# A ConvNeXt-V2 block on one core: two-bank expansion tiles, the evacuation last in a slot, statistics one slot later, and means aggregated by bn_stats

## The chip, the core and the metric

The kernel runs on one core of a Trainium2 chip. The metric is the device time of one execution in microseconds (us). Inputs and outputs are in bf16, and sums are formed in f32.

## The reference

The input `x` is one image of 512 x 512 pixels with 96 channels. All of it is one ConvNeXt-V2 block:

```python
out = sum over i, j of xp[:, i:i+H, j:j+W, :] * dw[i, j]     # 3x3 depthwise, zero padding
h = layernorm(out)                                           # over the 96 channels, eps 1e-5
h = gelu_tanh(einsum('bhwc,ce->bhwe', h, w1))                # 96 -> 384
gx = sqrt((h * h).sum(axis=(1, 2)) + 1e-6)                   # over all pixels, one per channel
nx = gx / (gx.mean(axis=-1) + 1e-6)
h = grn_gamma * (h * nx) + grn_beta + h
return x + einsum('bhwe,ec->bhwc', h, w2)                    # 384 -> 96
```

`gx` needs the squares of all activated values of the whole image before the last product can begin, so the kernel makes two passes.

## The kernel before

**Blocks and slots.** The image is cut into 128 blocks of four rows (2048 pixels). The first pass is one Python loop over slots `s`. In each slot several blocks are at different stages; a table filled by `put(slot, stage, block)` says which. Engines take their instructions in the order in which the loop issues them (the class `InOrder`, line 35, through which nearly every instruction goes; that is why the profile shows L35 for nearly all), so this order is written out by hand. In the steady part a slot does the following, each for another block.

- SP issues loads of `x` (`load_x`), reads of normalized rows (`stage_read`, `ynT`), writes of them (`stage_write`, `yn_dram`), the small row transfers of the layer norm (`stage_rows`, `stage_bcast`, tile `rbc`), and a third of a stored block (`store_next`).
- POOL: `stage_newton` (eight small operations for a batch of four blocks), `stage_norm` (`yn = y_bf * rbc`), `stage_sq` (`ysq = y_bf * y_bf`, of the block whose convolution was evacuated in the slot before), `stage_rstd` (four small operations for a batch).
- PE: the 3x3 convolution of block `s` as 72 matmuls on 64x32 tiles, issued in three bursts `conv(0)`, `conv(1)`, `conv(2)` into the three banks `Y3`; a PE drain follows `conv(0)`. `evac` on ACT copies `Y3` to `y_bf`. `stage_stats` takes 24 small matmuls (`rowsel`) over `y_bf` and `ysq`, the sums for the layer norm.
- PE and ACT: the expansion to 384 channels and the gelu of one block, 12 banks of 512 numbers, by `unit(bank, n)`: `n` banks are filled by matmuls of `w1p` and `ynT`, and one ACT instruction turns them to `g`.
- DVE: `turn_x` (two transposes of x, tile `xT`); `stage_moments` (reads the sums, then clears the bank); `squares`, `squares_rest` and `square_owed`, which issue one `bn_stats` on 512 numbers each into `bst`. `bn_stats` writes six numbers: count, mean and sum of squared deviations of the even and of the odd elements. The rest of the block is squared on PE by `gram_next`.

The PSUM banks: `banks(2)` is always banks 0 and 1, and `banks(1)` takes banks 2 and 3 in turn. `Y3` is banks 4 to 6, bank 7 holds the sums `S` and the gram matrix. In a slot with expansion the order is

```python
conv(0)
unit(0, 2); unit(2, 1); squares(0)
conv(1, False)
spread_out(); turn_x(s + 3)
unit(3, 1); unit(4, 2); squares(1); gram_next(1)
unit(6, 1); squares(2); unit(7, 1)
stage_turn; conv(2); evac(); gram_next(1)
unit(8, 2); unit(10, 1); stage_stats; unit(11, 1); stage_moments
squares_rest(2); square_owed()
```

**Aggregation.** Every 32 entries of `bst` (a group) are put together by three `bn_aggr`, one for each 128 channels, into mean and variance `mv`. `second_moments` turns these to sums of squares `parts`. After the loop the last group and the gram matrix are added and the scale for `w2` is formed; this is the gate between the passes.

**Second pass.** 14 tail blocks at the end of the first pass go through `mlp_tail`, with tiles of three banks. The output pass then recomputes, keeps or loads `g`, multiplies by the scaled `w2` and adds `x`.

Of the kernel before, what the change touches and what calls it, by code (L numbers as in the profile page):

```python
# [8 lines left out]
ALU = mybir.AluOpType  # L9
ACTF = mybir.ActivationFunctionType  # L10
AX = mybir.AxisListType
# [3 lines left out]
GRN_EPS = 1e-6  # L15
# [41 lines left out]
def kernel(  # L57
# [92 lines left out]
    NLAST = cm_quads(NBLK - 2) + cm_quads(NBLK - 1)  # L150
    GROUPS = [min(32, NENT - k) for k in range(0, NENT, 32)] + [NLAST]
    NACC = len(GROUPS)
    mv = consts.tile([128, NCH, NACC, 2], f32, name="mv")
    parts = consts.tile([128, NCH, NACC + 1], f32, name="parts")
    npx = consts.tile([128, NACC], f32, name="npx")
    grp = {}
    NYT = 6
    yn_ring = [prepool.tile([128, GR, W], bf16, name=f"ynT{i}") for i in range(NYT)]
# [25 lines left out]
    with ExitStack() as p1:  # L184
# [2 lines left out]
        ones = [0]  # L187

        def banks(n):
            if n == 2:  # L190
                return PS[:, 0:2, :]
            ones[0] += 1
            return PS[:, 2 + ones[0] % 2:3 + ones[0] % 2, :]

        threes = [0]

# [183 lines left out]
        def busy(n):  # L380
            for k in range(n):
                pe.matmul(Y3[:, k % NI, :], lhsT=zrow[:, :128], rhs=zrow[:], start=True, stop=True)
# [16 lines left out]
        n = 0  # L399
# [35 lines left out]

        def setup_rest():
            dve.memset(ones_f[:], 1.0)
            for k in range(NACC):
                dve.memset(npx[:, k:k + 1], float(GROUPS[k] * QW))
            dve.tensor_copy(out=gam[:], in_=gam_bf[:])  # L440

        def turn_x(b):
# [64 lines left out]
        def stage_sq(b, on_act):  # L507
            q = ysqpool.tile([128, NI, W], bf16, name="ysq")
            if on_act:
                act.activation(out=q[:], in_=ybf[b][:], func=ACTF.Square)  # L510
            else:
                pool.tensor_tensor(out=q[:], in0=ybf[b][:], in1=ybf[b][:], op=ALU.mult)
            ysq[b] = q
# [242 lines left out]
        def square_owed():  # L756
            while owed:
                owed.pop()()
# [10 lines left out]

        def aggregate(k):  # L770
            bst = bsts.pop(k)
            for j in range(NCH):
                dve.bn_aggr(out=mv[:, j, k, :], in_=bst[:, j, :GROUPS[k], :].rearrange("p a s -> p (a s)"))

        def combine(b):
            for k in sorted(bsts):
# [1 line left out]
                    aggregate(k)  # L778

        def second_moments(k0, k1):  # L780
            v, p = mv[:, :, k0:k1, :], parts[:, :, k0:k1]
            dve.tensor_tensor(out=p, in0=v[:, :, :, 0], in1=v[:, :, :, 0], op=ALU.mult)
            dve.tensor_tensor(out=p, in0=p, in1=v[:, :, :, 1], op=ALU.add)
            dve.tensor_tensor(out=p, in0=p, in1=npx[:, None, k0:k1].to_broadcast([128, NCH, k1 - k0]), op=ALU.mult)

        at = {}

# [6 lines left out]
        for k, (b0, n) in enumerate(BATCHES):  # L794
# [16 lines left out]
            for b in range(b0, b0 + n):  # L811
# [7 lines left out]
                put(m + is_whole(b), "combine", b)  # L819
                last_slot = m  # L820

        busy(FILL[1])
        turn_x(0)
        turn_x(1)
        turn_x(2)
        for s in range(last_slot + 1):
            get = lambda kind: at.get((s, kind), [])
            if s + 4 < NBLK:
                load_x(s + 4)
            for b in get("read"):  # L830
                stage_read(b)
            for b in get("write"):
                stage_write(b)
            for k in get("bcast"):
                stage_bcast(k)
            for k in get("rows"):
                stage_rows(k)
            store_next()
            for k in get("newton"):
                stage_newton(k, pool)  # L840
            for b in get("norm"):
                stage_norm(b)
            for b in get("sqp"):
                stage_sq(b, False)
            for k in get("rstd"):
                stage_rstd(k, pool)
            mlp = get("mlp")

            def spread_out():
                for k in get("spread"):  # L850
                    stage_spread(k)
                for b in get("norma"):
                    stage_norm(b, dve if b < 2 else pool)

            spare = not mlp and s % 2 == 1
            taps, evac = conv_taps(s, spare) if s < NBLK else ([], None)
            if mlp and mlp[0] >= TAIL0:
                assert not taps
                square_owed()
                mlp_tail(mlp[0], get)  # L860
            elif not mlp:
                if s + 3 < NBLK:
                    turn_x(s + 3)
                for f in taps:
                    f()
                if not spare:
                    spread_out()
                if evac:
                    evac()
                for b in get("sqa"):  # L870
                    stage_sq(b, True)
                for b in get("stats"):
                    stage_stats(b)
                for k in get("moments"):
                    stage_moments(k)
                if spare:
                    spread_out()
                for k in get("chain"):
                    stage_moments(k)
                    stage_chain(k)  # L880
                for k in get("turn"):
                    stage_turn(k)
                gram_next(2)
                square_owed()
            else:
                b = mlp[0]
                unit, squares, squares_rest = mlp_units(b)
                conv = lambda n, fence=True: taps[n](fence) if taps else None

                conv(0)  # L890
                unit(0, 2)
                unit(2, 1)
                squares(0)
                conv(1, False)
                spread_out()
                if s + 3 < NBLK:
                    turn_x(s + 3)
                unit(3, 1)
                unit(4, 2)
                squares(1)  # L900
                gram_next(1 if taps else 2)
                unit(6, 1)
                squares(2)
                unit(7, 1)
                for k in get("turn"):
                    stage_turn(k)
                conv(2)
                if evac:
                    evac()
                gram_next(1 if taps else 2)  # L910
                unit(8, 2)
                unit(10, 1)
                for b2 in get("stats"):
                    stage_stats(b2)
                unit(11, 1)
                for k in get("moments"):
                    stage_moments(k)
                squares_rest(2)
                square_owed()
                if is_whole(b):  # L920
                    owed.append(lambda f=squares_rest: f(3))
                grams.extend((b, c) for c in range(cm_quads(b) * QC, NQ * QC, 2 * E))
                if is_whole(b):
                    stores.extend((b, h) for h in range(3))
            if s == 0:
                setup_ynt()
            if s == 3:
                setup_mlp()
            if s == 4:
                setup_rest()  # L930
            for b in get("combine"):
                combine(b)
            if s == last_slot - 3:
                pc.close()
                late.xr = p2.enter_context(tc.tile_pool(name="xr", side="right", bufs=5))
                late.xb = p2.enter_context(tc.tile_pool(name="xb", side="right", bufs=3))
                late.gr = p2.enter_context(tc.tile_pool(name="gr", side="right", bufs=GRB))
                late.gl = p2.enter_context(tc.tile_pool(name="gld", side="right", bufs=2))
                late.o = p2.enter_context(tc.tile_pool(name="o", side="right", bufs=4))
            if s == last_slot - 2:  # L940
                for n in range(PRE):
                    load_xr(n, sp)
            if s == last_slot - 1:
                for n in range(3):
                    stage_xb(ORDER[n], pool, B2bc_f)
                second_moments(0, NACC - 1)
            if s == last_slot:
                for n in range(PRE):
                    load_rest(n, sp, sp)
# [5 lines left out]
        aggregate(NACC - 1)  # L955
        second_moments(NACC - 1, NACC)
        sums = gsm.tile([128, NCH], f32, name="sums")
        dve.tensor_reduce(out=sums[:], in_=parts[:, :, :NACC], axis=AX.X, op=ALU.add)
        for j in range(NCH):
            junk = bstpool.tile([128, 128], f32, name="junk")  # L960
            dve.scalar_tensor_tensor(out=junk[:], in0=gram[:, j, :], scalar=1.0, in1=ident_f[:],
                                     op0=ALU.mult, op1=ALU.mult, accum_out=parts[:, j, NACC:NACC + 1])
        ssq = gsm.tile([128, NCH], f32, name="ssq")
        dve.scalar_tensor_tensor(out=ssq[:], in0=sums[:], scalar=GRN_EPS, in1=parts[:, :, NACC],
                                 op0=ALU.add, op1=ALU.add)
        gi = gsm.tile([128, NCH], i32, name="gi")
        dve.tensor_scalar(out=gi[:], in0=ssq[:].bitcast(i32), scalar1=-0.5, scalar2=float(0x5F3759DF),
# [84 lines left out]
```

## Time and profile before

| What | Value |
|---|---|
| Three runs | 1476.99, 1479.7, 1480.79 us; median 1479.7 |
| The profiled execution: its span, which is also its time as given | 1480.8 us |
| Granted TensorE clock, mean | 0.994 |
| First pass, from the first y_bf to the last (start) | 12.1 to 883.7 us |
| Gate (last aggregation to scaled w2) | 967.1 to 973.5 us |
| Busy: PE, DVE, ACT, POOL | 1391.3, 1182.0, 1414.4, 1300.3 us |
| ACT, g of one bank, of two banks | x684, mean 701 ns; x342, mean 1115 ns |
| ACT, y_bf of three banks | x121, mean 1561 ns |
| DVE, bn_stats on 512 numbers | x1110, mean 672 ns |
| DVE, bn_aggr on 32 entries | x33, mean 978 ns |
| POOL, yn and ysq | x126, mean 3108 ns; x114, mean 2752 ns |

Means are lengths of single instructions. On ACT, PE and DVE the next one starts before the last has ended, so the price of an instruction on a full engine is the distance from its start to the next start, which the timeline shows; it is less than the mean length.

### The profile page before, as it was taken

How to read it: one execution, taken by the hardware profiler on the slowest of the kernel's cores; microseconds unless marked ns; L12 is line 12 of the kernel's file. 1: busy time of each engine (PE TensorE's matmuls, PEld its weight loads, DVE VectorE, ACT ScalarE, POOL GpSimd, SP SyncE). 2: the span in 40 equal slices, each digit the busy share in tenths (PEclk: the TensorE clock that was granted, in tenths of full speed). 3: DMA queues.
4: the chain of work that ended last, by engine and by line, in shares of the span. 5: the costliest groups of instructions: out<-in, count | busy, mean ns of one | idle time of the engine just before them, and what ended most of it. 6: DMA issues, size and time to landing. Idle time of an engine off the chain costs nothing.

```text
span 1480.8 us, 54225 instructions
## 1 busy us (share of the span) xinstructions
PE 1391.3 (94%) x23125; PEld 810.4 (55%) x23125; DVE 1182.0 (80%) x2135; ACT 1414.4 (96%) x1595; POOL 1300.3 (88%) x922
## 2 busy tenths in 40 slices
PE   8888999999999999999999997789999999999998
PEld 3434444444444444444444445467777777776776
DVE  7849989999999999999999987965555555555555
ACT  7888989999999999999999999999999999999997
POOL 3459889998998999998999987569999999999997
PEclk9999999999999999999999999999999999999999
DMA  5568788788888888888888866669999999999997
GB/s 180 179 205 255 241 253 280 228 271 260 260 248 264 258 264 255 276 253 254 263 258 266 263 216 195 195 225 409 366 359 402 417 416 413 419 410 417 411 412 282
DMA packets 167768, 433.08 MB, mean 292 GB/s; under 512 B 31558, under 2 KB 81318, under 8 KB 163046
## 3 DMA queue, kind: packets, MB, share of 16 engines
q1 hardware_dynamic: 151284, 326.04, 66.3%
q0 software_dynamic: 14880, 103.43, 17.6%
q8 instruction: 181, 2.97, 0.8%
q14 instruction: 61, 0.50, 0.1%
q10 hardware_dynamic: 1362, 0.15, 0.1%
HBM read 273.30 MB, written 156.22 MB: 290 GB/s over the span
## 4 chain that ended last, share of the span: by engine, by line
PE 30%; ACT 24%; DMA 19%; POOL 13%; DVE 6%; issue 4%; SPq 4%; POOLq 0%; ACTq 0%; DVEq 0%
PE PS L35 30%; ACT g L35 16%; DMA out_dram<-o_sb 9%; POOL yn L35 6%; ACT y_bf L35 5%; POOL ysq L35 5%; SPq L35 4%; DMA yn_dram<-yn 3%; DVE bst L35 3%; DMA xin<-in_x_dram 2%; DMA rbc<-r_dram 2%; DMA ynT<-yn_dram 1%; DMA g_dram<-g 1%; DVE o_sb L35 1%; ACT xT L35 1%
## 5 line engine op out<-in xcount | busy, mean ns | idle before, releaser
L35 ACT ACTIVATE g<-PS 128x512 bf16<-128x512 f32 (+2 forms) x1062 | 727.7, 864 | 16.5 <-PE PS L35 15.6
L35 DVE BATCH_NORM_STATS2 bst<-g 128x6 f32<-128x512 bf16 x1110 | 671.3, 672 | 35.4 <-ACT g L35 34.5
L35 PE MATMUL PS<-ynT,w1p 128*128 128x512 bf16 x2181 | 609.6, 381 | 23.6 <-ACT g L35 5.4
L35 ACT ACTIVATE gr<-PS 128x1536 bf16<-128x1536 f32 x360 | 498.5, 1459 | 18.8 <-PE PS L35 13.8
L35 POOL TENSOR_TENSOR yn<-y_bf,rbc 128x1536 bf16<-128x1536 bf16 x126 | 391.3, 3108 | 77.3 <-ACT rbc L35 21.9
L35 DVE TENSOR_TENSOR o_sb<-PS,xb 128x384 bf16<-128x384 f32 x512 | 277.3, 556 | 227.0 <-PE PS L35 190.1
L324 POOL TENSOR_TENSOR xb<-xr,B2c 128x1536 f32<-128x1536 bf16 x118 | 368.1, 3133 | 4.3 <-DVE o_sb L35 2.0
L35 PE MATMUL PS<-xT,Wq 64*32 64x511 bf16 (+1 forms) x9198 | 340.5, 389 | 26.2 <-ACT y_bf L35 8.1
L35 POOL TENSOR_TENSOR ysq<-y_bf 128x1536 bf16<-128x1536 bf16 x114 | 313.6, 2752 | 12.8 <-ACT y_bf L35 12.8
L35 PEld LDWEIGHTS <-w1p 128*128 128x128 bf16 x2181 | 171.6, 98 | 222.0 <-issue 133.4
L35 PEld LDWEIGHTS <-gr 128*128 128x128 bf16 x4296 | 212.1, 98 | 68.9 <-issue 12.0
L35 PE MATMUL PS<-W2s,gr 128*128 128x96 bf16 x4224 | 223.5, 206 | 8.2 <-DVE o_sb L35 8.0
L35 PEld LDWEIGHTS <-Wq 64*32 64x32 bf16 x9216 | 111.9, 90 | 193.3 <-issue 145.9
L35 ACT ACTIVATE y_bf<-PS 128x1536 bf16<-128x1536 f32 (+2 forms) x135 | 199.4, 1482 | 17.4 <-PE PS L35 13.3
L35 DVE STREAM_TRANSPOSE xT<-xin 128x576 f32<-128x576 f32 (+1 forms) x256 | 181.4, 748 | 8.1 <-DMA xin<-in_x_dram 8.1
L35 PEld LDWEIGHTS <-g 128*128 128x128 bf16 x1704 | 104.9, 98 | 86.3 <-issue 54.3
L35 PE MATMUL PS<-w1p,ynT 128*128 128x256 bf16 (+2 forms) x822 | 125.8, 273 | 8.0 <-ACT xT L35 3.2
L35 PE MATMUL PS<-g 128*128 128x128 bf16 x1464 | 122.6, 220 | 2.9 <-DVE PS L35 2.6
L35 PEld LDWEIGHTS <-gl 128*128 128x128 bf16 x1680 | 82.8, 98 | 26.8 <-issue 5.0
L35 PE MATMUL PS<-W2s,gl 128*128 128x96 bf16 x1680 | 89.5, 206 | 3.4 <-DVE o_sb L35 3.2
L35 PEld LDWEIGHTS <-ynT 128*128 128x128 bf16 x822 | 64.1, 97 | 31.5 <-issue 13.7
L279 POOL DMA_DIRECT2D xr<-in_x_dram x115 | 63.7, 555 | 14.2 <-POOL xb L324 14.2
(105 smaller groups left out, 576.5 us busy)
## 6 DMA issues: line engine op xcount, KB each, us to landing
xin<-in_x_dram SPq DMA_DIRECT2D x126, 432.0 KB
g_dram<-g SPq DMA_DIRECT2D x105, 512.0 KB
gl<-g_dram POOLq DMA_DIRECT2D x35, 1536.0 KB, 11.3
yn_dram<-yn SPq DMA_DIRECT2D x512, 96.0 KB
ynT<-yn_dram SPq DMA_DIRECT2D x128, 384.0 KB
out_dram<-o_sb SPq DMA_DIRECT2D x127, 384.0 KB
xr<-in_x_dram POOLq DMA_DIRECT2D x123, 384.0 KB, 6.9
ynT<-yn_dram SPq DMA_DIRECT2D x85, 512.0 KB
```

What stands on the lines that cost most here:

```text
L35: r = f(*a, **k)
L279: pq.dma_start(out=xr[:], in_=x[0, r0:r0 + GR].rearrange("r w c -> (r w) c").rearrange("(p g) c -> p g c", g=PXP))
L324: pq.tensor_tensor(out=xb[:], in0=grp[q]["xr"][:], in1=bias[:, None, :].to_broadcast([128, PXP, C]), op=ALU.add)
```

## The change

Five things are changed.

1. `banks(n)` gives banks 0-1 and banks 2-3 in turn, whatever `n` is. In a steady slot the expansion becomes six units of two banks in place of nine of two, one and one.
2. The order in a slot: two units come first, then the statistics (and moments) that the slot before left over, a gram, and only then `conv(0)`. `conv(1)` stands between units 4 and 6, and `conv(2)` with `evac` after the last unit. `spread_out` moves from behind `conv(1)` to behind the last unit.
3. `stage_stats` and `stage_moments` of a slot are kept in lists and issued by `flush_stats` in the next one.
4. On POOL the squares are issued before the norms, and `stage_rstd` after the expansion.
5. A group is aggregated by three `bn_stats` over its 64 means and one `tensor_reduce` over its 64 sums of squared deviations, in place of three `bn_aggr`. `second_moments` has two operations more, and the 13 memsets of `npx` go.

```diff
         def banks(n):
-            if n == 2:
-                return PS[:, 0:2, :]
             ones[0] += 1
-            return PS[:, 2 + ones[0] % 2:3 + ones[0] % 2, :]
+            k = 2 * (ones[0] % 2)
+            return PS[:, k:k + n, :]
...
         def aggregate(k):
             bst = bsts.pop(k)
+            n = 2 * GROUPS[k]
+            v = bst[:].rearrange("p j e (h s) -> p j (e h) s", h=2)[:, :, :n]
             for j in range(NCH):
-                dve.bn_aggr(out=mv[:, j, k, :], in_=bst[:, j, :GROUPS[k], :].rearrange("p a s -> p (a s)"))
+                dve.bn_stats(out=mom2[:, j, k].rearrange("p h s -> p (h s)"), in_=v[:, j, :, 1])
+            dve.tensor_reduce(out=tot2[:, k, :], in_=v[:, :, :, 2], axis=AX.X, op=ALU.add)
...
         def second_moments(k0, k1):
-            v, p = mv[:, :, k0:k1, :], parts[:, :, k0:k1]
-            dve.tensor_tensor(out=p, in0=v[:, :, :, 0], in1=v[:, :, :, 0], op=ALU.mult)
-            dve.tensor_tensor(out=p, in0=p, in1=v[:, :, :, 1], op=ALU.add)
-            dve.tensor_tensor(out=p, in0=p, in1=npx[:, None, k0:k1].to_broadcast([128, NCH, k1 - k0]), op=ALU.mult)
+            v, p = mom2[:, :, k0:k1], parts[:, :, k0:k1]
+            dve.tensor_tensor(out=p, in0=v[:, :, :, :, 1], in1=v[:, :, :, :, 1], op=ALU.mult)
+            dve.tensor_tensor(out=p, in0=p, in1=v[:, :, :, :, 0], op=ALU.mult)
+            dve.tensor_tensor(out=p, in0=p, in1=v[:, :, :, :, 2], op=ALU.add)
+            dve.tensor_scalar(out=p, in0=p, scalar1=float(QW // 2), scalar2=None, op0=ALU.mult)
+            dve.tensor_tensor(out=p[:, :, :, 0], in0=p[:, :, :, 0],
+                              in1=tot2[:, k0:k1, :].rearrange("p k j -> p j k"), op=ALU.add)
...
+        late_stats, late_moments = [], []
+
+        def flush_stats():
+            for b2 in late_stats:
+                stage_stats(b2)
+            ks = list(late_moments)
+            del late_stats[:], late_moments[:]
+            return ks
...
+            for b in get("sqp"):
+                stage_sq(b, False)
             for b in get("norm"):
                 stage_norm(b)
-            for b in get("sqp"):
-                stage_sq(b, False)
-            for k in get("rstd"):
-                stage_rstd(k, pool)
...
+                unit(0, 2)
+                unit(2, 2)
+                squares(0)
+                for k in flush_stats():
+                    stage_moments(k)
+                gram_next(1)
                 conv(0)
-                unit(0, 2)
-                unit(2, 1)
-                squares(0)
-                conv(1, False)
-                spread_out()
                 if s + 3 < NBLK:
                     turn_x(s + 3)
-                unit(3, 1)
                 unit(4, 2)
                 squares(1)
-                gram_next(1 if taps else 2)
-                unit(6, 1)
+                conv(1, False)
+                unit(6, 2)
                 squares(2)
-                unit(7, 1)
+                unit(8, 2)
+                gram_next(1)
                 for k in get("turn"):
                     stage_turn(k)
+                unit(10, 2)
+                spread_out()
                 conv(2)
                 if evac:
                     evac()
-                gram_next(1 if taps else 2)
-                unit(8, 2)
-                unit(10, 1)
-                for b2 in get("stats"):
-                    stage_stats(b2)
-                unit(11, 1)
-                for k in get("moments"):
-                    stage_moments(k)
+                late_stats.extend(get("stats"))
+                late_moments.extend(get("moments"))
                 squares_rest(2)
                 square_owed()
...
+            for k in get("rstd"):
+                stage_rstd(k, pool)
```

Slots without expansion and the first slot of the tail also issue `flush_stats` at their head.

More of the change, by code (lines that the diff above doesn't have):

```diff
@@ L152 @@
     NACC = len(GROUPS)
-    mv = consts.tile([128, NCH, NACC, 2], f32, name="mv")
-    parts = consts.tile([128, NCH, NACC + 1], f32, name="parts")
-    npx = consts.tile([128, NACC], f32, name="npx")
+    mom2 = consts.tile([128, NCH, NACC, 2, 3], f32, name="mom2")
+    tot2 = consts.tile([128, NACC, NCH], f32, name="tot2")
+    parts = consts.tile([128, NCH, NACC, 2], f32, name="parts")
+    dsum = consts.tile([128, NCH], f32, name="dsum")
     grp = {}
@@ L437, in setup_rest @@
             dve.memset(ones_f[:], 1.0)
-            for k in range(NACC):
-                dve.memset(npx[:, k:k + 1], float(GROUPS[k] * QW))
             dve.tensor_copy(out=gam[:], in_=gam_bf[:])
@@ L859 @@
                 square_owed()
+                for k in flush_stats():
+                    stage_moments(k)
                 mlp_tail(mlp[0], get)
             elif not mlp:
+                for k in flush_stats():
+                    stage_moments(k)
                 if s + 3 < NBLK:
@@ L888 @@
                 conv = lambda n, fence=True: taps[n](fence) if taps else None
-                conv(0)
-                unit(0, 2)
-                unit(2, 1)
-                squares(0)
-                conv(1, False)
-                spread_out()
+                unit(0, 2)
+                unit(2, 2)
+                squares(0)
+                for k in flush_stats():
+                    stage_moments(k)
+                gram_next(1)
+                conv(0)
                 if s + 3 < NBLK:
                     turn_x(s + 3)
-                unit(3, 1)
                 unit(4, 2)
                 squares(1)
-                gram_next(1 if taps else 2)
-                unit(6, 1)
+                conv(1, False)
+                unit(6, 2)
                 squares(2)
-                unit(7, 1)
+                unit(8, 2)
+                gram_next(1)
                 for k in get("turn"):
                     stage_turn(k)
+                unit(10, 2)
+                spread_out()
                 conv(2)
@@ L957 @@
         sums = gsm.tile([128, NCH], f32, name="sums")
-        dve.tensor_reduce(out=sums[:], in_=parts[:, :, :NACC], axis=AX.X, op=ALU.add)
+        dve.tensor_reduce(out=sums[:], in_=parts[:].rearrange("p j k h -> p j (k h)"), axis=AX.X, op=ALU.add)
         for j in range(NCH):
@@ L961 @@
             dve.scalar_tensor_tensor(out=junk[:], in0=gram[:, j, :], scalar=1.0, in1=ident_f[:],
-                                     op0=ALU.mult, op1=ALU.mult, accum_out=parts[:, j, NACC:NACC + 1])
+                                     op0=ALU.mult, op1=ALU.mult, accum_out=dsum[:, j:j + 1])
         ssq = gsm.tile([128, NCH], f32, name="ssq")
-        dve.scalar_tensor_tensor(out=ssq[:], in0=sums[:], scalar=GRN_EPS, in1=parts[:, :, NACC],
+        dve.scalar_tensor_tensor(out=ssq[:], in0=sums[:], scalar=GRN_EPS, in1=dsum[:],
                                  op0=ALU.add, op1=ALU.add)
```

## The prediction

> **What bounds the kernel now.** The page comes first: parts 1 and 2 say that for the first 24 of 40 slices PE, DVE, ACT and POOL are all at eight or nine tenths, so no engine can be called the bound from its share alone.
>
> ```profile
> PE 1391.3 (94%) x23125; PEld 810.4 (55%) x23125; DVE 1182.0 (80%) x2135; ACT 1414.4 (96%) x1595; POOL 1300.3 (88%) x922
> ...
> DVE  7849989999999999999999987965555555555555
> ACT  7888989999999999999999999999999999999997
> ```
>
> From slice 25 on (output stage) the change touches nothing. What matters is one slot of the main loop, so I read the timeline of ACT over two slots next. Columns: start, length (us), operation, count.
>
> ```profile
> 500.20 1.51 ACT L35 ACTIVATE y_bf<-PS 128x1536 bf16<-128x1536 f32 x1
> 501.53 5.87 ACT L35 ACTIVATE g<-PS 128x1024 bf16<-128x1024 f32 x9
> 507.12 1.61 ACT L35 ACTIVATE y_bf<-PS 128x1536 bf16<-128x1536 f32 x1
> 508.46 5.97 ACT L35 ACTIVATE g<-PS 128x1024 bf16<-128x1024 f32 x9
> ...
> 513.72 0.71 ACT L35 ACTIVATE g<-PS 128x512 bf16<-128x512 f32 x1
> 514.19 1.58 ACT L35 ACTIVATE y_bf<-PS 128x1536 bf16<-128x1536 f32 x1
> 515.52 5.94 ACT L35 ACTIVATE g<-PS 128x1024 bf16<-128x1024 f32 x9
> 521.25 1.55 ACT L35 ACTIVATE y_bf<-PS 128x1536 bf16<-128x1536 f32 x1
> ```
>
> Instructions overlap, so their price is the distance between starts. y_bf costs 501.53 - 500.20 = 1.33; a one-bank g costs 514.19 - 513.72 = 0.475; nine without a gap take 507.12 - 501.53 = 5.59, so a two-bank g costs (5.59 - 6 x 0.475) / 3 = 0.91. ACT's own sum is 6.93 a slot; y_bf to y_bf is 6.92, 7.07, 7.06, mostly 7.03. The missing 0.1 is found on PE, in its timeline (columns as before, the bracket is idle time and its releaser):
>
> ```profile
> 507.00 0.81 PE L35 MATMUL PS<-ynT,w1p 128*128 128x512 bf16 x3
> 507.65 0.45 PE L35 MATMUL PS<-rowsel,y_bf 128*128 128x4 bf16 x12
> 507.96 0.44 PE L35 MATMUL PS<-rowsel,ysq 128*128 128x4 bf16 x12
> 508.26 0.38 PE L35 MATMUL PS<-ynT,w1p 128*128 128x512 bf16 x1
> 508.79 0.88 PE L35 MATMUL PS<-xT,Wq 64*32 64x512 bf16 x24 [0.15 <-ACT y_bf L35]
> ...
> 515.82 0.89 PE L35 MATMUL PS<-xT,Wq 64*32 64x512 bf16 x24
> 516.83 0.82 PE L35 MATMUL PS<-ynT,w1p 128*128 128x512 bf16 x3
> 517.58 0.87 PE L35 MATMUL PS<-xT,Wq 64*32 64x512 bf16 x24
> 518.38 0.85 PE L35 MATMUL PS<-ynT,w1p 128*128 128x512 bf16 x3
> 519.07 0.50 PE L35 MATMUL PS<-g 128*128 128x128 bf16 x6
> 519.40 0.59 PE L35 MATMUL PS<-ynT,w1p 128*128 128x512 bf16 x2
> 519.92 0.89 PE L35 MATMUL PS<-xT,Wq 64*32 64x512 bf16 x24
> ```
>
> PE waits for ACT's y_bf, then ACT waits for PE. Prices by distance of starts: first taps with their drain 515.82 to 516.83, 1.01; second 517.58 to 518.38, 0.80; two expansion matmuls and the change to 64x32 tiles 519.40 to 519.92, 0.52 (0.43 + 0.09); gram 0.33; statistics 507.65 to 508.26, 0.61. From the start of unit(0) to its activation: 509.77 to 510.46, 0.69. The loop of before is y_bf (1.57 + 0.05 to be seen) + taps 1.01 + 0.69 + activations 0, 2, 3, 4, 6, 7 (2 x 0.91 + 4 x 0.475 = 3.72) = 7.04, against 7.03 measured. The method holds.
>
> DVE stands equally near: its timeline has 549.98 to 556.64 for two transposes and nine statistics, 6.66, plus 0.45 of moments and 0.15 of rt in every fourth slot, plus 2.68 of three bn_aggr (539.38 to 542.06) in every 10.7th: 7.06. POOL: by starts yn 3.07 and ysq 2.71 a slot, and 4.5 of small operations in every fourth: 6.9.
>
> **The change, part by part.**
>
> *Wider tiles.* Six activations of 0.475 become three of 0.91: 3 x (0.95 - 0.91) = 0.12 less a slot; ACT's sum falls to 6 x 0.91 + 1.33 = 6.79. But the four banks now hold two tiles in turn instead of three (two banks, one, one). Unit n+2 may start on PE only when activation n has ended.
>
> *New order.* Count from the start of y_bf, t = 0. Activation 10 started 0.91 earlier and lasts 1.115 (mean of its row), so its banks are free at 0.25. Unit(2): 0.25 to 0.68. Statistics: 1.29. Gram: 1.62. Tile change: 1.71, and there the first taps start (y_bf is seen at 1.62, so it is no longer the last to come). Taps end 2.72. Unit(4), whose banks activation 0 freed at 2.5, and the tile change: 3.24. Second taps: 4.04. Unit(6) is ready 0.69 later, 4.73. ACT, with nothing to wait for, would have wanted it at 1.33 + 3 x 0.91 = 4.06: it idles 0.67 in all before activations 4 and 6. Then activations 6, 8, 10: 3 x 0.91 = 2.73, and y_bf at 7.46. The third taps do not hold it: unit(10) starts when activation 6 ends (4.73 + 1.12 + 0.05 = 5.90), and 0.52 + 0.82 + 0.26 ends at 7.5 at the most, 7.4 with the 1.09 that an activation after a wait lasts (510.46). The slot comes out at 7.40 to 7.46; I take 7.42.
>
> A floor that does not depend on the head: were unit(4) early, its banks come free at 2.5, second taps end at 2.5 + 0.52 + 0.80 = 3.82, unit(6) is ready at 4.51, and the slot is 7.24. With activations of 1.07 it is 7.19.
>
> The Trainium skill, page Perfetto Trace Analysis, section Optimizing Scalar/DVE Operations, puts Scalar's cost per instruction at about 51 ns on PSUM and advises larger operations where the engine is saturated; ACT's 96% looks like that, and the sum by it would be 3 x 0.05 x 110 = 17 us less (an estimate from the page). [...]
>
> *Slots.* The by-form view has 684 one-bank activations, six a slot: 114 slots; four lie in the ramp (39.9 to 68.8 us), 110 follow. From y_bf at 99.14 to the last at 883.75 are 784.6 us for 110 intervals, 11.3 above 110 x 7.03: these are stalls of the POOL, rbc and SP chain (one of 3.3 near 690, one of 5.2 near 125, small ones).
>
> *Statistics and moments later.* Their 24 matmuls are on the path, and counted. DVE's moments queue behind squares(0): ready about 4.2 into the slot; POOL needs them after ysq and yn, at 1.6 + 2.7 + 3.1 = 7.4. Cover 3.2; without it POOL's 4.5 us chain moves back, and with it rt, the row DMAs on SP and rbc.
>
> *Squares before norms, rstd after the units.* POOL's order stays newton, one pair, rstd; the square now waits for a y_bf that comes last in its slot, with yn queued behind it, and SP's yn writes behind that. POOL has 6.9 of work in 7.42, so this costs nothing, and statistics find ysq ready where before they waited 10.2 us in all. I credit half to two thirds of the 11.3 us of stalls: 7. No DMA is added; SP's issues keep their order, reads stay two slots ahead.
>
> *Aggregation.* 33 bn_aggr of 978 ns (11 groups) go. For bn_stats on 64 strided numbers no row exists: above the 0.17 us of a 128x3 operation, below the 0.59 of 512 numbers; I take 0.2, as the 128x64 transpose (229 ns). The reduce: 0.2 to 0.6, I take 0.3. So 0.9 for 2.68, 1.8 less, 20 us of DVE in all (3 to 22 by the bounds). DVE falls to 6.9 a slot, below the slot either way: credited at nothing. At the gate (967.08) three short bn_aggr of 0.19 become four operations and two more follow: +0.6 us on the path. Thirteen memsets go from set-up, uncovered at most 1 us.
>
> *Ramp.* Spread and its norm move behind unit(10) in one of four slots: 0 to 3 us; I take 1. Tail units (ACT busy 74.8 of 80 us) and output keep their instructions.
>
> **Sum.** 110 x (7.42 - 7.03) = 42.9; stalls -7; ramp and gate +1.6; minus 1 for the memsets: +36.5 on this execution's 1480.8, 1517. The median shown is 1.1 below the span; and the method was 0.01 to 0.02 high on before, 2 us. I give 1514.
>
> **Rivals.**
>
> *The two tiles suffice* (faster). If the second taps fitted behind a waiting activation, ACT would run at 6.79, and POOL's 6.9 would be next: 110 x 0.13 = 14 less and a few us of stalls, 1463. For it: PE no longer waits for y_bf at the head, and DVE gets its 0.17 a slot. Against: it needs ready times of units 4 and 6 at most 0.91 apart, and 0.52 + 0.80 = 1.32 lies between them. Only a burst of 0.39 or less decides for it. 0.10.
>
> *Only the buffer floor binds.* Statistics and gram overlap the wait better than I think; slot 7.19 to 7.24, less up to 11 of stalls: 110 x 0.16 - 11 = +7 to 110 x 0.21 - 5 = +18, 1487 to 1498. 0.10.
>
> *The square becomes the last to come.* Each late ysq now delays taps and ACT. Before waited 2.0 a time (10.2 in 5). Once in four slots: 27 x 2 = 54 on top, 1568. Against: POOL's slack. 0.04.
>
> **How the numbers follow.** Forecast 0.76: slots of 7.30 to 7.55 with stalls kept or gone give 1500 to 1535. The rest of the range goes to the buffer floor, whose lower half I leave out with both ends. Range 1489 to 1536. A measurement here can tell 0.3%, 4.4 us. Slower by more than that: 0.76 + 0.10 + 0.04 = 0.90, less 0.03 for a floor that loses its gain elsewhere, which is the chance of no change: 0.87, 0.03, and 0.10 for faster.
>
> **What would show it.** y_bf to y_bf near 7.4; six g activations of two banks with gaps before the third and fourth; ACT's waits on PE over 50 us where 15.6 stand; DVE and POOL with idle time in every slot; no wait of PE for ysq. It is wrong if the slot stays under 7.1, or ACT runs without gaps.

## The result, and the profile after

| Kernel | Median of runs (us) | Ratio to the kernel before, 95% interval | Profiled execution, span (us) |
|---|---|---|---|
| before | 1478.35 | | 1480.8 |
| changed | 1629.3 | 1.1025 [1.0981, 1.1069] | 1623.7 |

The change costs 10%, 143 us between the two profiled executions. The forecast was slower by 2.4%, 1514 us, with a range up to 1536: the direction was right, the size far off.

The page of the changed kernel, the lines that answer to those shown of before:

```profile
PE 1447.3 (89%) x23125; PEld 820.9 (51%) x23125; DVE 1175.1 (72%) x2139; ACT 1411.7 (87%) x1253; POOL 1303.8 (80%) x922
...
DVE  8658887888878888788878887686555555455555
ACT  7778788888788887888878888899999999899997
```

DVE, ACT and POOL are busy for nearly as long as before (within 7 us) and have lower shares: they wait. PE alone is busy for 56 us more, with as many instructions, so its instructions became longer. The output stage (from slice 28 on) is what it was.

The timeline of ACT over two slots and a half (start, length, operation, count, idle time before it and its releaser):

```profile
572.73 1.47 ACT L35 ACTIVATE y_bf<-PS 128x1536 bf16<-128x1536 f32 x1
574.06 1.97 ACT L35 ACTIVATE g<-PS 128x1024 bf16<-128x1024 f32 x2
579.76 1.02 ACT L35 ACTIVATE g<-PS 128x1024 bf16<-128x1024 f32 x1 [3.73 <-PE PS L35]
581.72 2.85 ACT L35 ACTIVATE g<-PS 128x1024 bf16<-128x1024 f32 x3 [0.93 <-PE PS L35]
584.45 1.47 ACT L35 ACTIVATE y_bf<-PS 128x1536 bf16<-128x1536 f32 x1
585.78 2.97 ACT L35 ACTIVATE g<-PS 128x1024 bf16<-128x1024 f32 x3
589.07 2.85 ACT L35 ACTIVATE g<-PS 128x1024 bf16<-128x1024 f32 x3 [0.32 <-PE PS L35]
591.79 1.47 ACT L35 ACTIVATE y_bf<-PS 128x1536 bf16<-128x1536 f32 x1
```

There are two kinds of slot. The second, 584.45 to 591.79, is the one that was forecast: 7.34, with ACT idle before activations 4 and 6 (the first of these gaps, 0.13 by the starts, is below what the view marks). The first, 572.73 to 584.45, is 11.72 and was not forecast. From the start of y_bf at 109.04 to the last at 1031.18 there are 26 such slots, 11.83 on average, one for each batch of four blocks; the others have a median of 7.35.

PE in the long slot:

```profile
573.63 0.44 PE L35 MATMUL PS<-rowsel,ysq 128*128 128x4 bf16 x12
576.94 0.49 PE L35 MATMUL PS<-g 128*128 128x128 bf16 x6 [2.87 <-DVE PS L35]
577.37 1.22 PE L35 MATMUL PS<-xT,Wq 64*32 64x512 bf16 x24
578.69 1.03 PE L35 MATMUL PS<-ynT,w1p 128*128 128x512 bf16 x2
579.65 1.48 PE L35 MATMUL PS<-xT,Wq 64*32 64x512 bf16 x24
581.06 1.05 PE L35 MATMUL PS<-ynT,w1p 128*128 128x512 bf16 x4
```

The gram waits 2.87 us for DVE, and afterwards everything on PE is slow. The first burst takes 577.37 to 578.69, 1.32 in place of 1.01; two expansion matmuls with the tile change 0.96 in place of 0.52; the second burst 579.65 to 581.06, 1.41 in place of 0.80. That is 1.4 us on top of 2.9. The windows of one microsecond say why; columns are window, length, busy time and instructions of PE, PEld, DVE, ACT and POOL, then the granted PE clock, DMA share, GB/s:

```profile
576.00:577.00 1.00, 0.06 (x2) 0.06 (x2) 0.90 (x4) 0.03 (x1) 1.00 (x1) 1.00 0.92 309
577.00:578.00 1.00, 1.00 (x30) 0.51 (x29) 1.00 (x2) 0.00 (x0) 1.00 (x2) 0.85 1.08 397
578.00:579.00 1.00, 0.90 (x17) 0.13 (x2) 1.00 (x3) 0.00 (x0) 1.00 (x1) 0.50 1.04 382
579.00:580.00 1.00, 1.00 (x10) 0.15 (x16) 0.37 (x1) 0.24 (x1) 1.00 (x1) 0.50 1.01 402
580.00:581.00 1.00, 1.00 (x24) 0.17 (x8) 0.18 (x1) 0.78 (x1) 0.83 (x4) 0.50 0.49 198
581.00:582.00 1.00, 1.00 (x13) 0.47 (x6) 1.00 (x2) 0.28 (x1) 0.83 (x3) 0.94 0.81 269
```

The clock is 1.00 while PE stands, and 0.50 when it works again, for some 3.4 us. It is not so in every long slot. Of the 26, 24 have a stretch at 0.50: 18 of 3.41 us (slots of 11.5 to 11.8) and six of 6.83 us (slots of 12.6 to 12.7). Two, at 474 and 744 us, have the same halt, 2.87 and 2.86 us, and keep a clock of 1.00; they last 10.36 and 10.33:

```profile
475.30:478.72 3.42, 1.63 (x32) 0.68 (x31) 3.32 (x7) 0.76 (x1) 3.42 (x2) 1.00 0.79 256
```

And DVE, for which the gram waits:

```profile
575.14 1.29 DVE L35 BATCH_NORM_STATS2 bst<-g 128x6 f32<-128x512 bf16 x2 [0.59 <-ACT g L35]
576.35 0.27 DVE L35 TENSOR_SCALAR mom<-PS 128x128 f32<-128x128 f32 x1
576.72 0.17 DVE L35 MEMSET PS<- 128x128 f32 x1
```

The sums are complete on PE at 574.07, the end of the rowsel row. DVE reads them only at 576.35, since the two bn_stats of squares(0) stand ahead in its queue and wait for activation 0.

### The profile page after: what moved, and what is told of

The parts are those of the page before. It is cut to its first block, busy times and chain, and to the rows that moved or that the text cites. A ratio compares the mean times of both kernels' runs of the same rounds, so it can differ in the third digit from the quotient of the medians.

```text
span 1623.7 us, 53890 instructions
## 1 busy us (share of the span) xinstructions
PE 1447.3 (89%) x23125; PEld 820.9 (51%) x23125; DVE 1175.1 (72%) x2139; ACT 1411.7 (87%) x1253; POOL 1303.8 (80%) x922
## 4 chain that ended last, share of the span: by engine, by line
PE 50%; ACT 12%; POOL 12%; DMA 12%; issue 7%; DVE 4%; SPq 2%; ACTq 0%; POOLq 0%; DVEq 0%
PE PS L35 50%; ACT g L35 9%; DMA out_dram<-o_sb 7%; POOL yn L35 7%; POOL xb L324 3%; SPq L35 2%; ACT y_bf L35 2%; DVE bst L35 2%; DMA yn_dram<-yn 2%; DMA ynT<-yn_dram 1%; POOL nt L35 1%; DVE o_sb L35 1%; ACT xT L35 1%; DMA rbc<-r_dram 1%; POOL var L35 1%
## 5 line engine op out<-in xcount | busy, mean ns | idle before, releaser
L35 ACT ACTIVATE g<-PS 128x1024 bf16<-128x1024 f32 (+1 forms) x720 | 713.4, 1064 | 158.3 <-PE PS L35 158.3
L35 DVE BATCH_NORM_STATS2 bst<-g 128x6 f32<-128x512 bf16 x1110 | 683.3, 676 | 185.4 <-ACT g L35 185.4
L35 PE MATMUL PS<-xT,Wq 64*32 64x511 bf16 (+1 forms) x9198 | 362.5, 410 | 8.2 <-ACT y_bf L35 3.0
L35 ACT ACTIVATE y_bf<-PS 128x1536 bf16<-128x1536 f32 (+2 forms) x135 | 188.2, 1399 | 21.0 <-PE PS L35 16.6
L35 PEld LDWEIGHTS <-Wq 64*32 64x32 bf16 x9216 | 104.6, 92 | 172.2 <-issue 126.9
L35 PEld LDWEIGHTS <-ynT 128*128 128x128 bf16 x822 | 74.9, 100 | 89.5 <-issue 70.3
```

What stands on the lines that cost most here:

```text
L35: r = f(*a, **k)
```

## The experiments

The theory after this trace: in `flush_stats` and the lines behind it the moments of a batch (DVE reads the sums and clears them) are issued ahead of the gram (PE). Both use PSUM bank 7, so the gram waits for the clear, with the convolution and the rest of the slot queued behind it on PE; after the halt PE's clock is halved in most cases. The other part, the slot of 7.34 in place of 7.03, is put down to two tiles in turn. In the text below a slot is the distance between starts of y_bf in the trace. The kernel before was measured again beside each group of runs. Its medians there were 1487.19 us (gram ahead, wait filled, three tiles), 1483.17 (moments ahead, two tiles in the old order, the two with the aggregation) and 1486.0 (the two cut bursts), against 1478.35 above. So times of different groups are compared by their ratios to it or by slots, and a few us between groups mean nothing.

**The gram ahead of the moments.** Changed kernel with

```diff
-                for k in flush_stats():
-                    stage_moments(k)
+                ks = flush_stats()
                 gram_next(1)
+                for k in ks:
+                    stage_moments(k)
                 conv(0)
```

> Theory (a wait in bank 7): in every fourth slot the gram at the head is issued behind the moments of a batch, shares PSUM bank 7 with them, and so PE stands 2.9 us until DVE has cleared the sums; PE then runs 3.4 us at a granted clock of 0.55, which costs another 1.5 us. With the gram ahead of the moments the slots of 11.7 us become slots of 7.35: 27 x 4.4 = 119 us less than the changed kernel's 1624, so about 1505 to 1512, with no wait of PE for DVE and the clock near 0.99. Rival (the batch work itself): the fourth slot is long because moments, the rstd chain and rt of a batch fall into it on DVE and POOL; the gram is only where PE notices. Then slots of 10 us or more stay, and the time stays above 1600.

Measured: 1507.58 us, ratio to before 1.0137 [1.0104, 1.017]. From 104.09 on no slot is above 7.94, the median is 7.34, the mean clock 0.996. The theory holds: one line's place is worth 117 us between the profiled executions (1623.7 and 1506.3), 122 between the medians. Two slots of the run on ACT:

```profile
506.47 1.47 ACT L35 ACTIVATE y_bf<-PS 128x1536 bf16<-128x1536 f32 x1
507.80 2.97 ACT L35 ACTIVATE g<-PS 128x1024 bf16<-128x1024 f32 x3
511.11 2.85 ACT L35 ACTIVATE g<-PS 128x1024 bf16<-128x1024 f32 x3 [0.34 <-PE PS L35]
513.84 1.47 ACT L35 ACTIVATE y_bf<-PS 128x1536 bf16<-128x1536 f32 x1
```

**The wait filled with work.** Changed kernel; between the moments and the gram, in slots with moments, `busy(10)`: ten matmuls of zeros into `Y3`, which the first burst overwrites later.

```diff
-                for k in flush_stats():
+                ks = flush_stats()
+                for k in ks:
                     stage_moments(k)
+                if ks:
+                    busy(10)
                 gram_next(1)
```

> The wait of the gram is left as it is, and ten unused matmuls of 512 columns into the three banks of the convolution fill it, in the slots with moments alone. If PE's clock falls because PE stands still, it now stays near 0.99 in these slots and they take about 10.2 us in place of 11.7: 27 x 1.5 = 40 us less, about 1584. If the half clock has another reason, or if the long matmuls behind the wait are no more than a late start, the time stays at 1624 or rises by what the ten matmuls reach over the wait (at most 0.5 us a time, 13 us).

Measured: 1589.45 us, 40 less than the changed kernel by the medians and 38 between the profiled executions. PE in a long slot (the record has nine of the ten matmuls):

```profile
489.90 2.32 PE L35 MATMUL PS<-zrow 128*128 128x512 bf16 x9 [0.17 <-ACT y_bf L35]
492.60 0.49 PE L35 MATMUL PS<-g 128*128 128x128 bf16 x6 [0.38 <-DVE PS L35]
493.03 0.87 PE L35 MATMUL PS<-xT,Wq 64*32 64x512 bf16 x24
```

The gram starts as late as before, yet the clock stays at 1.00, and the 26 long slots are 10.35 on average in place of 11.83, as long as the two of the changed kernel that kept their clock. Of the 4.5 us that a long slot takes over a short one, 3.0 are the wait and 1.5, on average, the half clock, which did not come once PE was kept at work.

**The moments ahead of squares(0).** Changed kernel; `squares(0)` is moved behind the loop over `flush_stats()`, and the gram stays behind the moments.

```diff
-                squares(0)
                 for k in flush_stats():
                     stage_moments(k)
+                squares(0)
                 gram_next(1)
```

> The changed kernel with squares(0) issued on DVE behind the moments in place of ahead of them; the gram still waits for the cleared bank. In the trace of the changed kernel the sums are complete at 574.1, DVE has ended its old work at 574.55, but the moments start at 576.35, behind two bn_stats that wait for activation 0. Without these PE should wait 1.1 us in place of 2.9 in every fourth slot: 27 x 1.8 = 49 us less. If a wait this short leaves the clock alone, another 40 us less: about 1535; if the clock halves all the same, about 1575. If the gram does not wait for DVE's clear, as the rival to the first theory has it, the time stays at 1624.

Measured: 1542.07 us, ratio 1.039 [1.0366, 1.0415], 7 above the 1535 of a clock left alone. Such a wait is shown on PE as

```profile
380.83 0.49 PE L35 MATMUL PS<-g 128*128 128x128 bf16 x6 [0.97 <-DVE PS L35]
```

and the long slots are 8.5. The clock of the whole execution is 0.997, and no stretch at 0.50 follows any of these halts, most of about 1.0 us and two of 1.74 and 1.76. The wait follows DVE's order of work, as the theory has it.

**Three tiles in the new order.** The gram ahead of the moments, `banks` of before, and units (0,2), (2,1), (3,1), (4,2), (6,1), (7,1), (8,2), (10,1), (11,1); the second burst stands between units 6 and 7.

```diff
-                unit(2, 2)
+                unit(2, 1)
+                unit(3, 1)
...
                 unit(4, 2)
                 squares(1)
+                unit(6, 1)
                 conv(1, False)
-                unit(6, 2)
                 squares(2)
+                unit(7, 1)
...
```

> The gram is ahead of the moments as in the run before, and the expansion goes back to three tiles (two banks, one, one) in the new order: evacuation last, statistics at the next head. Theory (two tiles are too few for the burst between units 4 and 6): the gaps of ACT before units 4 and 6 go, the slot falls from 7.35 to about 7.0, and the time to about 1470 to 1480. Rival (the order itself makes the slot 7.35, because statistics and gram stand between the evacuation and the first burst): the slot stays at 7.2 or more and the time at 1495 or more.

Measured: 1488.21 us, ratio 1.001 [0.9981, 1.0038] to before. The slot is 7.03 again. The new order costs nothing with three tiles, and gains nothing either: by the ratio it is as fast as the kernel before, whose median beside it was 1487.19. The time is 8 above the top of what was expected. The wait in bank 7 is part of this: now the second gram of a slot is at times ready before DVE has cleared the sums, and PE stands for 11.4 us in 12 waits between 103 and 889 us, in slots of 7.7 to 8.3 for the most part.

**Two tiles in the old order.** Kernel before, `banks` of after, units of two banks, and a drain behind the second burst.

```diff
                 conv(0)
                 unit(0, 2)
-                unit(2, 1)
+                unit(2, 2)
                 squares(0)
-                conv(1, False)
+                conv(1)
...
```

> The kernel before with units of two banks in turn in banks 0-1 and 2-3, its order kept, and a PE drain behind the second burst as behind the first, because with fewer units nothing else orders the second burst before the third; the drain makes it 1.0 in place of 0.8 us. Theory (two tiles are too few): unit(2) can start only when activation 10 has ended, the second burst follows it, unit 4 is ready 0.4 us after ACT wants it; slot 7.3 to 7.45, of which the drain is 0.2; time 1508 to 1525. Rival (the order is what loses): ACT's gain of 0.14 a slot shows, the drain lies beside it, slot 7.1 or less, time at most 1487.

Measured: 1503.42 us, ratio 1.0127 [1.0101, 1.0153]; slot 7.31. The time is some 5 us below the range that was expected, the slot within its range. The pairs in the old order lose too, but this run does not say how much of it is due to the tiles: the drain lengthens the second burst from 0.80 to 0.99 just ahead of the one gap of ACT that the view marks (0.33 before activation 4), so of the 0.28 over the slot of before up to 0.19 can be the drain, and at least 0.09 is left for the pairs. No run has pairs in the old order without the drain.

```profile
405.77 0.86 PE L35 MATMUL PS<-xT,Wq 64*32 64x512 bf16 x24
406.76 0.60 PE L35 MATMUL PS<-ynT,w1p 128*128 128x512 bf16 x2
...
407.40 1.02 ACT L35 ACTIVATE g<-PS 128x1024 bf16<-128x1024 f32 x1 [0.33 <-PE PS L35]
```

**Which burst is on the loop.** Two kernels with the gram ahead of the moments, each with one burst cut from 24 to 8 matmuls, so part of the convolution is missing (the first of them is shown; the other has `mms[2]`):

```diff
+            if not spare:
+                mms[1] = mms[1][:8]
             flat = [m for ms in mms for m in ms]
```

> Left out on purpose: 16 of the 24 matmuls of the second burst of the convolution (in slots with expansion, and in the other slots that are not spare), so part of the convolution is missing. Otherwise the kernel with the gram ahead of the moments, whose slot is 7.34. Theory (the second burst lies between units 4 and 6 on the loop that sets the slot, since only two tiles are in turn): the burst is 0.43 us shorter, unit 6 is ready when ACT wants it, the slot falls to 6.95 to 7.0, time 1464 to 1470. Rival (PE as a whole is too full in the new order): the same as in the next run, where as many matmuls are left out of the third burst.

> Left out on purpose: 16 of the 24 matmuls of the third burst in place of the second. Theory: the third burst ends while activation 10 still runs, so it is not on the loop; the slot stays at 7.34, time 1503 to 1508, though PE has just as much less to do as in the run before. Rival (PE as a whole is too full): the slot falls by the same 0.35 to 0.4 us as there, 1464 to 1470.

Measured: 1480.83 us with a short second burst, slot 6.91; 1506.71 us with a short third burst, slot 7.34 as without the cut. Their ratios to the kernel before are 0.996 [0.9934, 0.9986] and 1.0157 [1.0131, 1.0182]. The same work taken from PE is worth 0.43 a slot in one place and nothing in the other. ACT with the short second burst, then with the short third:

```profile
505.41 1.49 ACT L35 ACTIVATE y_bf<-PS 128x1536 bf16<-128x1536 f32 x1
506.74 5.71 ACT L35 ACTIVATE g<-PS 128x1024 bf16<-128x1024 f32 x6
512.32 1.48 ACT L35 ACTIVATE y_bf<-PS 128x1536 bf16<-128x1536 f32 x1
```

```profile
506.37 2.97 ACT L35 ACTIVATE g<-PS 128x1024 bf16<-128x1024 f32 x3
509.64 2.86 ACT L35 ACTIVATE g<-PS 128x1024 bf16<-128x1024 f32 x3 [0.31 <-PE PS L35]
```

In the first, six activations run with no gap that the view marks; in the second the gap before activation 6 is still there. The time of the first run came out 11 to 17 above what was expected although the slot was met (6.91 against 6.95 to 7.0): from 201 us on, 11 single slots of 7.5 to 9.8 appear, 13 us in all above 6.91. In nine of them PE waits for DVE in bank 7 once more, 0.6 to 1.7 us, at the second gram of the slot. The one from 242.29 to 250.47:

```profile
247.94 0.30 DVE L35 TENSOR_SCALAR mom<-PS 128x128 f32<-128x128 f32 x1
248.34 0.17 DVE L35 MEMSET PS<- 128x128 f32 x1
248.56 0.50 PE L35 MATMUL PS<-g 128*128 128x128 bf16 x6 [1.32 <-DVE PS L35]
```

Nine bn_stats stand ahead of the moments on DVE there, and the clear ends 6.2 us into the slot. So with the first gram moved the shared bank is still a risk for the second. What would keep DVE on time was not tried.

**Aggregation alone.** Kernel before with `aggregate`, `second_moments` and what belongs to them from the changed kernel (the diff of them is the one in the section on the change).

> The kernel before with the aggregation by bn_stats and tensor_reduce alone. DVE loses about 1.8 us in each of 11 groups, 20 us in all. Theory (the loop of y_bf, first burst, unit(0) and six activations sets the slot of 7.03, and DVE's 7.06 only stands near it): the slot stays at 7.03 and the time within 5 us of the kernel before. Rival (DVE was the bound): the slot falls to about 6.95, as far as ACT's 6.93 lets it, and the time by 8 to 12 us.

Measured: 1484.84 us, ratio 1.0008 [0.9987, 1.0028]; slot 7.03. DVE was busy for 1166.2 us in place of 1182.0 and nothing moved: DVE's 7.06 a slot was not the bound.

**Aggregation and squares ahead of norms.** The run above and

```diff
+            for b in get("sqp"):
+                stage_sq(b, False)
             for b in get("norm"):
                 stage_norm(b)
-            for b in get("sqp"):
-                stage_sq(b, False)
```

> As the run above, with the squares ahead of the norms on POOL as well. The slot is set elsewhere, so only stalls can go: PE's 10 us of waiting for ysq should vanish, but yn comes 2.7 us later, and with it the writes, so stalls on rbc and yn can grow. Between 5 us less and 10 us more than the run above. If squares ahead of norms were harmful, more than 10 us more.

Measured: 1484.83 us, ratio 1.0013 [0.9992, 1.0034]. No difference. PE's wait for ysq falls from 11.6 us in 7 waits to 4.2 in 5; it was expected to vanish. The waits of POOL's yn on rbc are 41.1 us in 15, against 20.0 in 11 in the run above, and yet the time is the same.

## Why the prediction was wrong

**The loop of before: right.** DVE did not set the slot: the run with the aggregation alone shows it. That y_bf, first burst, unit(0) and six activations do is a sum that comes to 7.04, and it fits the trace. Half-way through the first pass (240 to 560 us) the only place in a slot where ACT's starts are farther apart than elsewhere by more than 0.02 is before activation 0, 0.59 on median in place of 0.48. With three tiles in the new order the same loop runs through unit(4), with six activations of the same sizes behind it, and the slot is the same.

**The slot of the new order: right, and a little high.** From the start of y_bf at 584.45, with the forecast's numbers in brackets: first burst 1.63 (1.71), unit(4) 2.64 (2.72), second burst 3.17 (3.24), unit(6) 3.97 (4.04), activation 6 4.62 (4.73), next y_bf 7.34 (7.42). What made it high, as far as the rows tell, is the length of the activation: 1.115 was the mean of rows in which instructions queue behind each other; after a wait it is 1.02, and the banks come free earlier. 110 x (7.34 - 7.03) = 34 us. That the second burst between units 4 and 6 makes it, the two cut bursts show; that two tiles are too few for it, the run with three tiles shows. The kernel with the gram ahead is the change without the wait, and its 1507.58 us lie near the forecast's 1514 and within its range.

**The step that failed: "Statistics and moments later".** It followed the moments from DVE to POOL and found 3.2 us of cover there. It did not ask who waits on PE. The gram that the change puts behind the moments got its price of 0.33 and no wait, though the code issues it after the clear of a bank that it shares; so the "new order" sum, which ran from statistics to gram without a gap, holds only for slots without moments. The two facts needed were in the code and the trace of before: bank 7 holds both `S` and `gram`, and PE already waited there for DVE. The waits of the whole execution (us, times, longest), before and after:

```profile
PE PS L35 <- DVE PS L35: 2.6, 4, 1.6
PE PS L35 <- DVE PS L35: 77.6, 29, 2.9
```

In the old order the moments stood behind the last unit, and PE's next instruction in bank 7 came only after two bursts and four units of the next slot: that was their cover. The forecast's own numbers would have given the wait: moments ready at 4.2 in the slot, gram due at 1.29, so 2.9, against 2.87 measured. 26 x 3.0 = 78 us for the wait and 26 x 1.5 = 39 for the clock, of which the forecast had neither. The half clock could be seen in the trace of before as well, if rarely. There PE stands for 3.98 us at 114 us and for 2.01 us at 691 us, each time for ysq, and 3.41 us at 0.50 follow both times. The second of these:

```profile
693.47 0.46 PE L35 MATMUL PS<-rowsel,ysq 128*128 128x4 bf16 x12 [2.01 <-POOL ysq L35]
...
696.49 1.48 PE L35 MATMUL PS<-xT,Wq 64*32 64x512 bf16 x24
697.90 1.05 PE L35 MATMUL PS<-ynT,w1p 128*128 128x512 bf16 x3
```

```profile
694.99:698.40 3.41, 3.31 (x31) 0.82 (x30) 3.41 (x7) 1.51 (x2) 3.41 (x2) 0.50 0.96 301
```

A burst takes 1.41 there in place of 0.80.

**The rival of the late square: wrong in its mechanism.** PE did lose time once in four slots, but by the clear of a bank, not by ysq.

**The small terms.** Stalls: 7 credited; with the gram moved the first pass from 104.09 to 910.49 takes 806.4 us, no more than 110 x 7.34, so nothing is left of the 11. Aggregation: three bn_stats of some 230 ns and a reduce of some 400 ns, by the starts 0.75 to 0.77 for a group against 0.9, off the path as said. Ramp: 1 given; the steady part begins 4.9 us later than before with the gram ahead (104.09 against 99.14), and 9.9 later in the changed kernel (109.04). What part of it is the move of spread was not tried.

**The sum by the runs.** The wait and its half clock: 1624 to 1506 between the profiled executions, 117 us. Two tiles in place of three: 1508 to 1488, 19 us; this is less than the 34 of the slots, since the run with three tiles has stalls again (785.0 us from 103.36 to 888.41, 12 above 110 x 7.03). Order with three tiles, aggregation and squares: nothing that a measurement here can tell. None of the runs that compute the whole is faster than the kernel before.

## What to carry to other kernels

When an instruction is moved ahead of another on a different engine, write down for each PSUM bank which engine touched it last and who is next in it: the price of a moved step is the wait of the next user of its bank, with all that is queued behind it. Moving one step away need not end it: the next user of the bank can be caught in its turn. Merging instructions lowers an engine's own sum, but with the same banks it also lowers the number of tiles in flight, here from three to two; compare the longest burst between two fills with one evacuation before counting the gain. A wait on PE can cost more than its length, here 4.5 us for one of 2.9 on average, so it pays to shorten it or to fill it.

## What the runs showed of the hardware

In the changed kernel 26 halts of PE of 2.9 us came in the long slots. After 24 of them the clock was 0.50, for 3.41 or 6.83 us; after two it was not. The same wait of the gram filled with nine or ten zero matmuls was not followed by 0.50, nor were halts of 1.0 us. Between these lengths the runs differ: 0.50 followed halts of 2.01 us in the kernel before and of 1.45 and 1.67 us in the run with a short second burst, and did not follow two of 1.74 and 1.76 us in the run with the moments ahead. So the length of a halt alone does not decide. In the changed kernel all slow stretches between 62 and 1018 us start at whole multiples of 3.413 us from each other, so that the place of a halt on this grid is likely to matter; which share of such a window must be idle was not found.

The Trainium skill, page TensorE: Matmul & The Clock Gate, part 1 (the HAM clock gate), says that the clock falls to half after at least one idle window of about 3.4 us and comes back after about as long a busy one. The length of the slow stretch agrees, 3.41 us or twice that. The windows ahead of the slow stretches were not idle here: in the one ahead of the stretch shown above (574.30 to 577.71 us) PE was busy for 0.77 us, and in others for up to 2.07 us. The measurement decides.
